# q and k turned into blocks of 32 adjacent values, with the order of time restored in products, masks and copies

## The chip, the cores and the metric

The kernel runs on one core of one Trainium2 chip. The core's engines run side by side, each with a queue of its own and tied to the others by semaphores: TensorE (PE, matrix products; its loads of the stationary operand are shown as PEld), VectorE (DVE), ScalarE (ACT), GpSimd (POOL), and SyncE (SP), which here only issues transfers. SBUF is the working memory of 128 partitions; PSUM holds TensorE's results. The metric is the device time of one execution in microseconds (us), lower is better. A profile is one execution recorded by the hardware profiler.

## The reference

Two blocks follow one another. The first is gated linear attention over 768 steps, for 4 sequences and 8 heads of 48 channels:

```python
for t in range(S):
    state = alpha[:, :, t, :, None] * state + np.einsum('bhd,bhe->bhde', k[:, :, t], v[:, :, t])
    y[:, :, t] = np.einsum('bhd,bhde->bhe', q[:, :, t], state)
```

The second takes y with the heads side by side, as x of 384 channels:

```python
proj = x @ w_in
val, gate = (proj[..., :D_inner], proj[..., D_inner:])
a = np.exp(A_log)[None, None, :]
h = np.zeros((B, D_inner), dtype=np.float32)
for t in range(S):
    h = a[0, 0] * h + val[:, t, :]
    ys[:, t, :] = h
silu = gate * (1.0 / (1.0 + np.exp(-gate)))
return (silu * ys @ w_out).astype(np.float32)
```

D_inner is 512. All inputs of the attention are fp32; the weights come as 64-bit floats and are converted on the chip.

## The kernel before

The 4 x 768 steps are cut into 12 groups of 256 steps (`GC`), numbered 0 to 11, three to a sequence. Everything is fp32. In SBUF, channels lie on partitions: heads 0 to 3 on partitions 0 to 47, heads 4 to 7 on 64 to 111, with 256 steps of each of the four heads of a half along the partition.

The recurrence becomes products. For a group, two scans on VectorE run over the gates alpha: P (line 635), the running product from the group's start, and V (line 654), from each step to the group's end, scaled by the reciprocal of the last P. The scaled queries Zq = q * P (`scaled_q`, line 610) and the scaled keys Zk = k * V (`scaled_k`, line 619) then go to TensorE:

- `scores` (line 797): for each head and each run of 64 steps (`L`), Zk is the stationary operand and Zq the moving one. In front of each 64 queries lie 48 columns of the identity, so one instruction of 112 columns gives the 64x64 scores and also turns k back to steps on partitions.
- `masks` (lines 807 to 817): the scores are multiplied by a triangular mask on VectorE or GpSimd into A, and the turned k is copied by ScalarE.
- `values` (line 831; for group 0 `first_values`, line 915): y from A and v. `carried` (line 844; group 0: line 923): y from the state before each run of 64 and Zq.
- `states` (line 863): the states' increments, summed by `add_up` on GpSimd (line 883) or `add_banks` on VectorE (line 891).
- `join` (lines 957 to 962; group 0: `first_join`): ScalarE copies y from PSUM; transfers issued by SyncE and GpSimd (line 960) bring each head to its place in xT, the input of the second block.
- `project` (line 981) multiplies xT with the weights, VectorE scans h from the result (`hh`, line 988), ScalarE makes the gate (line 999), VectorE or GpSimd multiplies both (line 1001). `output` (line 1015; for the last group line 1267) is the last product.

The inputs arrive with steps on partitions: partition c holds steps 8c to 8c+7 (`NJ` = 8 steps, 48 channels each, j counting the 8). Three ways turn them. Group 0's alpha and q have routines of their own on TensorE. Groups 0 to 2 of q and k, and alpha up to group 3, are turned by TensorE into PSUM and copied out by ScalarE (`turned` and `copy_turned`, lines 701 to 713). From group 3 for q and k, and group 4 for alpha, VectorE turns 32x32 blocks (`turn`, line 600): a block holds the 32 values of c for one j, and the result is written with 8 words between neighbours, so that the 256 steps lie in the order of time (8c + j).

The order of instructions on each engine is written out by hand in `fast`; every queue works in that order. `constants` fills, among others, the identity columns of the two Zq buffers (line 517) and the mask (line 524), both on GpSimd, and then issues the loads of group 0's v from GpSimd. For groups 0 and 2 `scaled_k` and `scaled_q` are called in halves (`c` = 0 and 1), each 512 values per partition; for all others whole, 1024 values. Weights are converted in between: by ScalarE (line 543), VectorE (lines 549 and 551) and GpSimd (line 556). Around this code stands a slower general version, taken only if the inputs are out of range; its instructions are not executed here.

Of the kernel before, what the change touches and what calls it, by code (L numbers as in the profile page):

```python
# [9 lines left out]
FP32 = mybir.dt.float32  # L10
# [3 lines left out]
AF = mybir.ActivationFunctionType  # L14
# [332 lines left out]
def fast(  # L347
# [39 lines left out]
    const = pool("const", 1)  # L387
    p1 = pool("p1", 1)
    p2 = pool("p2", 2)
# [4 lines left out]
    L = 64  # L394
    GP = GC + 1
    NJ = GC // 32
    ROW = NJ * D
    NQ = D + 16
    raws = {n: const.tile([C, 4 * ROW + 32], FP32, name=f"raw_{n}") for n in "aqk"}
# [83 lines left out]
    als = [const.tile([C, 4 * GP + 1], FP32, name=f"al{i}") for i in range(2)]  # L483
# [10 lines left out]
    def constants():  # L494
        make_identity(nc, ident)
        nc.vector.memset(wide_S[0], 0.0)
        for name in "aqk":
            for m in range(2):
                nc.vector.memset(steps_of(name, m)[:, 2 * ROW:], 1.0)
        for c in range(G):  # L500
            nc.vector.memset(wide[:, c].rearrange("p (h d) -> p h d", d=D)[:, 1::2, :], 0.0)
        for al in als:
            nc.vector.memset(al[:, ::GP], 0.0)
        nc.vector.memset(minus, -1.0)
        nc.vector.memset(one, 1.0)
        nc.vector.memset(lower, FLOOR)
        nc.vector.memset(lower[:, :, 0], FIRST_PRODUCT)
        nc.vector.memset(ends, 0.0)
        for t in wide_S[1:]:
            nc.vector.memset(t.rearrange("p (h d) -> p h d", d=D)[:, 1::2, :], 0.0)  # L510
        nc.scalar.activation(spare, minus, AF.Exp)
        for t in vs:
            nc.vector.memset(t[:, :, :, D:64], 0.0)
        for n, t in enumerate(Zqs):
            for i in range(2):
                rows = ds(64 * i, 64)
                nc.gpsimd.tensor_copy(out=t[rows, :, :, 0:D].rearrange("p u h d -> p (u h) d"),
                                      in_=ident[rows, None, ds(64 * i, D)].to_broadcast([64, 8 * G, D]))
            if n:
                nc.gpsimd.memset(tri, 1.0)  # L520
                nc.gpsimd.affine_select(out=tri, in_=tri, compare_op=ALU.is_ge, fill=0.0, base=0,
                                        channel_multiplier=-1, pattern=[[1, C]])
                for h in range(2):
                    nc.gpsimd.tensor_copy(out=mask[ds(L * h, L)], in_=tri[ds(L * h, L), ds(L * h, L)])
                load_v(0, nc.gpsimd)

    def bits_of(i):
# [65 lines left out]
    def by_place(t):  # L593
        return t[:, 0:4 * GP].rearrange("p (h t) -> p h t", h=4)

    def by_runs(t):
        return t.rearrange("p h (c j) -> p h c j", j=NJ)

    def turn(name, to):
        nc.vector.transpose(out=by_runs(to).rearrange("p h c j -> p h j c"),  # L600
                            in_=raws[name][:, 0:4 * ROW].rearrange("p (h j d) -> p h j d", h=4, d=D)
                            [:, :, :, 0:32])

    def plain(name):
        return p1.tile([C, 4, GC], FP32, tag=name, name=name)

    def scaled_q(m, t, P, c=None):
        u0, n = (0, 2 * G) if c is None else (2 * c, 2)
        at = ds(u0 * L, n * L)
        nc.vector.tensor_mul(Zqs[m % 2][:, ds(u0, n), :, D:].rearrange("p u h t -> p h u t"),  # L610
                             t[:, :, at].rearrange("p h (u t) -> p h u t", t=L),
                             P[:, :, 1:GP][:, :, at].rearrange("p h (u t) -> p h u t", t=L))

    def scaled_k(m, t, V, c=None):
        if not c:
            Zks[m] = p2.tile([C, G, 4, C], FP32, tag="Zk", name="Zk")
        c0, n = (0, G) if c is None else (c, 1)
        at = ds(c0 * C, n * C)
        nc.vector.tensor_mul(Zks[m][:, ds(c0, n)].rearrange("p c h t -> p h c t"),  # L619
                             t[:, :, at].rearrange("p h (c t) -> p h c t", t=C),  # L620
                             V[:, :, 1:GP][:, :, at].rearrange("p h (c t) -> p h c t", t=C))

    Zks = {}

# [85 lines left out]
    halves = [range(0, NJ // 2), range(NJ // 2, NJ)]  # L710

    def copy_turned(to, js, tp):
        nc.scalar.activation(by_runs(to)[:, :, :, js.start:js.stop], tp, AF.Copy)

    def first_alphas():
        raw, to = steps_of("a", 0), by_runs(by_place(als[0])[:, :, 1:GP])
# [66 lines left out]
    NS = S // L  # L783
    xTs, Ss, scs, sts, ys, partss = {}, {}, {}, {}, {}, {}

    def scores(m, cs=range(G)):
        Zk, Zq = Zks[m], Zqs[m % 2]
        for c in cs:
            scs.setdefault(m, []).append(bank_pair(None if c else "s"))
            if not c or not m:  # L790
                sts.setdefault(m, []).extend(scs[m][c])
            for p in range(4):
                for h in range(2):
                    u = 2 * c + h
                    for i in range(2):
                        rows = ds(64 * i, D)
                        nc.tensor.matmul(scs[m][c][i][ds(L * h, L), ds(p * (L + D), L + D)],  # L797
                                         Zk[rows, c, p, ds(h * L, L)], Zq[rows, u, p],
                                         start=True, stop=True, skip_group_check=True)

    def masks(m, cs=range(G)):
# [33 lines left out]
    def carried(m, us):  # L835
        for u in us:
            j = (m % NG) * 2 * G + u - 1
            if j < 0:
                continue
            for e in range(2):  # L840
                for s in range(2):
                    for i in range(2):
                        p, rows = 2 * e + (s ^ i), ds(64 * i, D)
                        nc.tensor.matmul(ys[m][i][ds(64 * s, 64), e, ds(u * L, L)], Ss[j][rows, p, :],  # L844
                                         Zqs[m % 2][rows, u, p, D:], start=False, stop=True,
                                         skip_group_check=True)

    def states(m):
# [69 lines left out]
    def first_carried(us):  # L918
        for u in us:
            for pair in zip(spread(0), spread(1)):  # L920
                for i, (p, at, to, e) in enumerate(pair):
                    rows = ds(64 * i, D)
                    nc.tensor.matmul(ys[0][i][to, e, ds(u * L, L)], wide_S[u - 1][rows, ds(at, L)],
                                     Zqs[0][rows, u, p, D:], start=False, stop=True, skip_group_check=True)

    def first_states(st):
        to = [t.rearrange("p (h d) -> p h d", d=D)[:, ::2, :] for t in wide_S]
# [3 lines left out]
        for u in range(1, 4):  # L931
            nc.vector.tensor_add(to[u], st[u % 2][u // 2], to[u - 1])

    def first_join():
        y = ys.pop(0)
        xT = xTs[0] = p2.tile([C, NK, GC], FP32, tag="xT", name="xT")
        nc.scalar.activation(xT[:, 0], y[0][:, 0], AF.Copy)
        nc.scalar.activation(xT[0:64, 1], y[0][0:64, 1], AF.Copy)
        nc.scalar.activation(xT[64:128, 1], y[1][64:128, 0], AF.Copy)
        nc.scalar.activation(xT[:, 2], y[1][:, 1], AF.Copy)  # L940

    moves = []
    for h in range(H):
        i, e, s = h // 4, h % 4 // 2, h % 2 ^ h // 4
        at = D * h
# [7 lines left out]
    def join(m, engines):  # L953
        y = ys.pop(m)
        st = p1.tile([C, 2, 2, GC], FP32, tag="yst", name="yst")
        xT = xTs[m] = p2.tile([C, NK, GC], FP32, tag="xT", name="xT")
        nc.scalar.activation(st[:, 0], y[0], AF.Copy)  # L957
# [89 lines left out]
    P = scan_P(0)  # L1047
# [3 lines left out]
    V = scan_V(0, P, False)  # L1051
# [17 lines left out]
    st = states(0)  # L1069
# [10 lines left out]
    P = scan_P(1)  # L1080
# [33 lines left out]
    for n in range(N):  # L1114
        m = n + 1
        if n == 0:
# [12 lines left out]
            P = scan_P(2)  # L1129
# [176 lines left out]
```

## Time and profile before

| | |
|---|---|
| time, median of 3 runs | 275.85 us (275.72 to 275.88) |
| profiled execution, span from first to last instruction | 274.0 us; the runs' median is 1.85 above it |
| PE busy | 269.2 us (98%), 4060 matrix products |
| DVE busy | 217.9 us (80%), 271 instructions |
| ACT busy | 109.5 us (40%) |
| POOL busy | 123.7 us (45%) |
| the chain that ended last | PE 91%, DVE 5%, ACT 1%, POOL 1%, issue 1% |

The profile gives no time of its own for the execution beside the span. A row of the groups reads: line, engine, operation, output<-inputs, shape, count | busy us in all, mean ns of one | us that the engine was idle just before them, and what ended it. A row of a timeline reads: start us, duration us, engine, line, operation, output<-inputs, count, and in brackets the idle time before it with what ended it. "PE busy" counts modelled ends of pipelined matrix products: products of one run overlap, so what a run costs is read from the start of one to the start of the next.

### The profile page before, as it was taken

The numbers are of one execution on the slowest core, as the hardware profiler recorded it, in microseconds if no ns is written. First come the engines' busy times: TensorE is split into PE (matmuls) and PEld (weight loads), VectorE is DVE, ScalarE is ACT, GpSimd is POOL, SyncE is SP. The second block draws the span as 40 slices with busy tenths as digits, with TensorE's granted clock in tenths as the row PEclk, the third lists the DMA queues.
The fourth block names the chain that finished last, engine by engine and source line by source line (L and its number), as shares of the span: only waits on it lengthen the run. The fifth ranks groups of instructions, "written<-read, shape, count | busy, mean of one in ns | idle before, by whom it ended". The sixth has DMA issues, their size and how long they took to land.

```text
span 274.0 us, 9640 instructions
## 1 busy us (share of the span) xinstructions
PE 269.2 (98%) x4060; PEld 216.8 (79%) x4060; DVE 217.9 (80%) x271; ACT 109.5 (40%) x252; POOL 123.7 (45%) x144
## 2 busy tenths in 40 slices
PE   8999999999999999999999999999999999999995
PEld 6988888876788687788688688688688787787884
DVE  7979998996798999694995995996995995873240
ACT  3668766451344333524424424425425415213111
POOL 8122223260237485385384485376376476334000
PEclk9999999999999999999999999999999999999999
DMA  6948975989639686684585595585596501201201
GB/s 173 319 141 263 265 169 160 260 174 226 167 97 229 162 192 147 178 190 119 151 204 135 150 208 137 143 208 138 137 214 144 138 0 31 73 1 38 70 2 60
DMA packets 52303, 41.18 MB, mean 150 GB/s; under 512 B 27392, under 2 KB 50944, under 8 KB 52256
## 3 DMA queue, kind: packets, MB, share of 16 engines
q1 hardware_dynamic: 49328, 37.34, 53.9%
q0 software_dynamic: 1536, 2.20, 3.0%
q10 hardware_dynamic: 1392, 0.99, 1.2%
q8 instruction: 33, 0.54, 0.9%
q14 instruction: 14, 0.11, 0.1%
HBM read 32.54 MB, written 4.72 MB: 136 GB/s over the span
## 4 chain that ended last, share of the span: by engine, by line
PE 91%; DVE 5%; issue 1%; ACT 1%; POOL 1%; DVEq 0%; POOLq 0%; ACTq 0%
PE mm L981 46%; PE mm L1015 21%; PE y L831 4%; PE y L844 4%; PE mm L797 3%; PE s L797 3%; PE s L863 3%; PE mm L1267 2%; DVE P L635 2%; PE mm L706 1%; PE y L778 1%; DVE V L654 1%; POOL w_in L556 1%; PE s L722 1%; DVE Zk L619 0%
## 5 line engine op out<-in xcount | busy, mean ns | idle before, releaser
L981 PE MATMUL mm<-xT,w_in 128*128 128x256 f32 x576 | 129.5, 382 | 0.1
L981 PEld LDWEIGHTS mm<-xT,w_in 128*128 128x128 f32 x576 | 107.9, 190 | 16.2 <-POOL w_in L556 0.4
L1015 PE MATMUL mm<-w_out,f_last 128*128 128x384 f32 x160 | 54.2, 492 | 0.0
L999 ACT ACTIVATE sg<-mm 128x256 f32<-128x256 f32 x48 | 18.4, 383 | 86.7 <-PE mm L981 86.6
L1001 POOL TENSOR_TENSOR f_last<-sg,hh 128x256 f32<-128x256 f32 x36 | 32.9, 917 | 33.4 <-ACT sg L999 19.9
L1015 PEld LDWEIGHTS mm<-w_out,f_last 128*128 128x128 f32 x160 | 29.7, 190 | 19.7
L883 POOL TENSOR_TENSOR sum<-sum,dS 128x192 f32<-128x192 f32 x30 | 30.3, 1010 | 21.4 <-ACT dS L871 11.9
L988 DVE TENSOR_TENSOR_SCAN hh<-a_dec,hh,mm 128x256 f32<-128x256 f32 x32 | 23.4, 731 | 14.5 <-PE mm L981 14.2
L635 DVE TENSOR_TENSOR_SCAN P<-al,lower 128x1028 f32<-128x1028 f32 x12 | 31.4, 2617 | 0.5
L654 DVE TENSOR_TENSOR_SCAN V<-al,ends 128x1028 f32<-128x1028 f32 x12 | 28.3, 2360 | 0.4
L960 POOL DMA_DIRECT2D xT<-yst x44 | 22.5, 517 | 12.6 <-ACT yst L957 11.3
L1009 ACT ACTIVATE o_sb<-mm 128x384 f32<-128x384 f32 x22 | 10.8, 490 | 37.4 <-PE mm L1015 37.4
L815 POOL TENSOR_TENSOR AK<-AK,mask 128x512 f32<-128x512 f32 x9 | 15.2, 1683 | 18.7 <-ACT AK L813 18.7
L812 DVE TENSOR_TENSOR A<-s,mask 128x256 f32<-128x256 f32 x9 | 3.8, 424 | 19.5 <-PE s L797 19.5
L556 POOL TENSOR_TENSOR w_in<-w_in,wr 128x768 int32<-128x768 int32 x4 | 7.3, 1825 | 25.6 <-DVE wr L551 16.1
L600 DVE STREAM_TRANSPOSE k<-raw_k 128x1024 f32<-128x1024 f32 x9 | 18.3, 2034 | 0.0
L600 DVE STREAM_TRANSPOSE q<-raw_q 128x1024 f32<-128x1024 f32 x9 | 18.2, 2019 | 0.0
L600 DVE STREAM_TRANSPOSE al<-raw_a 128x1024 f32<-128x1024 f32 x8 | 16.3, 2042 | 0.0
L619 DVE TENSOR_TENSOR Zk<-k,V 128x1024 f32<-128x1024 f32 (+1 forms) x14 | 16.1, 1150 | 0.1
L831 PEld LDWEIGHTS y<-AK,v 64*64 64x64 f32 x352 | 12.1, 134 | 5.1 <-issue 5.1
L610 DVE TENSOR_TENSOR Zq<-q,P 128x1024 f32<-128x1024 f32 (+1 forms) x14 | 14.8, 1056 | 0.1
L831 PE MATMUL y<-AK,v 64*64 64x64 f32 x352 | 14.5, 221 | 0.0
(163 smaller groups left out, 389.2 us busy)
## 6 DMA issues: line engine op xcount, KB each, us to landing
v<-in_v_dram SPq DMA_DIRECT2D x22, 192.0 KB, 3.4
out_dram<-o_sb SPq DMA_DIRECT2D x22, 192.0 KB, 2.5
raw_k<-in_k_dram SPq DMA_DIRECT2D x18, 184.0 KB, 3.4
raw_q<-in_q_dram SPq DMA_DIRECT2D x18, 184.0 KB, 3.8
raw_k<-in_k_dram SPq DMA_DIRECT2D x18, 176.0 KB, 3.7
raw_q<-in_q_dram SPq DMA_DIRECT2D x18, 176.0 KB, 4.0
wbits<-in_moe_w_in_dram SPq DMA_DIRECT2D x8, 384.0 KB, 5.7
raw_a<-in_alpha_dram SPq DMA_DIRECT2D x16, 184.0 KB, 5.0
```

The lines of the kernel that those rows point to most:

```text
L600: nc.vector.transpose(out=by_runs(to).rearrange("p h c j -> p h j c"), in_=raws[name][:, 0:4 * ROW].rearrange("p (h j d) -> p h j d", h=4, ...
L635: nc.vector.tensor_tensor_scan(out=P, data0=al[:, 0:4 * GP], data1=lower.rearrange("p h t -> p (h t)"), initial=0.0, op0=ALU.mult, op1=ALU ...
L654: nc.vector.tensor_tensor_scan(out=V[:, ::-1], data0=al[:, 1:4 * GP + 1][:, ::-1], data1=ends.rearrange("p h t -> p (h t)")[:, ::-1], init ...
L797: nc.tensor.matmul(scs[m][c][i][ds(L * h, L), ds(p * (L + D), L + D)], Zk[rows, c, p, ds(h * L, L)], Zq[rows, u, p], start=True, stop=True ...
L831: nc.tensor.matmul(ys[m][i][ds(64 * s, 64), e, ds(c * C + h * L, L)], v_sb[rows, c, 4 * i + p, :], As[i][rows, c, p, :], start=across and ...
L883: nc.gpsimd.tensor_add(Ss[j][:, :, 0:D], Ss[j - 1][:, :, 0:D], part)
L960: engines[n % len(engines)].dma_start(out=xT[to, a], in_=st[rows, i, e])
L981: nc.tensor.matmul((pv, pg)[vg], w_ins[cc][:, kk, vg, :], xT[:, kk, :], start=(kk == 0), stop=(kk == NK - 1))
L988: nc.vector.tensor_tensor_scan(out=hh, data0=a_dec[:, cc:cc + 1].to_broadcast([C, GC]), data1=pv, initial=prev_h[cc][:, GC - 1:GC] if n % ...
L999: nc.scalar.activation(sg, pg, AF.Silu)
L1001: f = lambda: engine.tensor_mul(fs[n][cc], sg, hh)
L1015: nc.tensor.matmul(os[c], fs[n][cc][:, ds(c * C, C)], w_outs[cc // 2][:, cc % 2, :], start=(cc == 0), stop=(cc == NI - 1))
```

## The change

q and k are no longer put in the order of time when they are turned. A turned tensor (`plain`) has the shape (head, j, c): for each of the 8 j the 32 values of c lie side by side, as the turn makes them. Alpha keeps the order of time, and so do P and V.

- `turn` writes its result as it comes for q and k; for alpha the caller passes the old pattern, steps of 8 words.
- `copy_turned` (ScalarE, out of PSUM) writes q and k in runs of 32 and reads PSUM in the other order.
- `scaled_k` multiplies the turned k, read across (one value, then the one 32 words on), with V in the order of time; Zk is in the order of time.
- `scaled_q` multiplies the turned q, read in runs, with P read 8 words apart. Zq keeps the order (j, c): 14 rows of 32 words for each head, 6 of identity columns and 8 of queries.
- A run of 64 steps is 8 neighbouring c for all 8 j, so `queries` gives TensorE 8 (or, with the identity, 14) runs of 8 words, 32 words apart. Within each 64 steps, the columns of the scores and of y are in the order (j, c).
- The mask gets its columns in that order. ScalarE's copies of y (`first_join`, `join`) read PSUM at steps of 8 words and write the order of time.
- The identity columns are written by 16 GpSimd copies of 192 values per partition instead of 4 of 768.

Number and order of the other instructions are as before on every engine. The diff, cut to its core:

```diff
-    Zqs = [const.tile([C, 2 * G, 4, L + D], FP32, name=f"Zq{i}") for i in range(2)]
+    Zqs = [const.tile([C, 4, NR + NJ, 32], FP32, name=f"Zq{i}") for i in range(2)]
...
-                nc.gpsimd.tensor_copy(out=t[rows, :, :, 0:D].rearrange("p u h d -> p (u h) d"),
-                                      in_=ident[rows, None, ds(64 * i, D)].to_broadcast([64, 8 * G, D]))
+                for u in range(2 * G):
+                    nc.gpsimd.tensor_copy(
+                        out=t[rows, :, 0:NR, ds(NJ * u, NJ)],
+                        in_=ident[rows, None, ds(64 * i, D)].to_broadcast([64, 4, D])
+                        .rearrange("p h (a c) -> p h a c", c=NJ))
...
-                    nc.gpsimd.tensor_copy(out=mask[ds(L * h, L)], in_=tri[ds(L * h, L), ds(L * h, L)])
+                    nc.gpsimd.tensor_copy(out=mask[ds(L * h, L)].rearrange("p (j c) -> p j c", j=NJ),
+                                          in_=tri[ds(L * h, L), ds(L * h, L)].rearrange("p (c j) -> p j c", j=NJ))
...
+    def of_runs(t):
+        return t.rearrange("p h (c j) -> p h j c", j=NJ)
+
     def turn(name, to):
-        nc.vector.transpose(out=by_runs(to).rearrange("p h c j -> p h j c"),
+        nc.vector.transpose(out=to,
...
-        return p1.tile([C, 4, GC], FP32, tag=name, name=name)
+        return p1.tile([C, 4, NJ, 32], FP32, tag=name, name=name)
...
-        nc.vector.tensor_mul(Zqs[m % 2][:, ds(u0, n), :, D:].rearrange("p u h t -> p h u t"),
-                             t[:, :, at].rearrange("p h (u t) -> p h u t", t=L),
-                             P[:, :, 1:GP][:, :, at].rearrange("p h (u t) -> p h u t", t=L))
+        at = ds(0, 32) if c is None else ds(16 * c, 16)
+        nc.vector.tensor_mul(Zqs[m % 2][:, :, NR:, at], t[:, :, :, at], of_runs(P[:, :, 1:GP])[:, :, :, at])
...
-            Zks[m] = p2.tile([C, G, 4, C], FP32, tag="Zk", name="Zk")
...
+            Zks[m] = p2.tile([C, 4, GC], FP32, tag="Zk", name="Zk")
+        at = ds(0, 32) if c is None else ds(16 * c, 16)
+        nc.vector.tensor_mul(by_runs(Zks[m])[:, :, at], t.rearrange("p h j c -> p h c j")[:, :, at],
+                             by_runs(V[:, :, 1:GP])[:, :, at])
...
-        turn("a", by_place(als[m % 2])[:, :, 1:GP])
+        turn("a", of_runs(by_place(als[m % 2])[:, :, 1:GP]))
...
-        nc.scalar.activation(by_runs(to)[:, :, :, js.start:js.stop], tp, AF.Copy)
+        if len(to.shape) == 3:
+            nc.scalar.activation(by_runs(to)[:, :, :, js.start:js.stop], tp, AF.Copy)
+        else:
+            nc.scalar.activation(to[:, :, js.start:js.stop], tp.rearrange("p h c j -> p h j c"), AF.Copy)
...
+    def queries(m, u, p, i, first=NR):
+        return Zqs[m % 2][ds(64 * i, D), p, first:, ds(NJ * u, NJ)]
...
-                                         Zk[rows, c, p, ds(h * L, L)], Zq[rows, u, p],
+                                         Zk[ds(64 * i, D), p, ds(u * L, L)], queries(m, u, p, i, 0),
...
-                                         Zqs[m % 2][rows, u, p, D:], start=False, stop=True,
+                                         queries(m, u, p, i), start=False, stop=True,
...
+    def steps_of_y(t):
+        return t.rearrange("p (u j c) -> p u c j", j=NJ, c=NJ)
+
+    def to_steps(t):
+        return t.rearrange("p (u c j) -> p u c j", j=NJ, c=NJ)
...
-        nc.scalar.activation(st[:, 0], y[0], AF.Copy)
-        nc.scalar.activation(st[:, 1], y[1], AF.Copy)
+        for i in range(2):
+            nc.scalar.activation(to_steps(st[:, i].rearrange("p e t -> p (e t)")),
+                                 steps_of_y(y[i].rearrange("p e t -> p (e t)")), AF.Copy)
...
-            nc.scalar.activation(xT[to, a], y[i][rows, e], AF.Copy)
+            nc.scalar.activation(to_steps(xT[to, a]), steps_of_y(y[i][rows, e]), AF.Copy)
```

More of the change, by code (lines that the diff above doesn't have):

```diff
@@ L396, in fast @@
     NJ = GC // 32
+    NR = D // NJ
     ROW = NJ * D
@@ L784, in fast @@
     xTs, Ss, scs, sts, ys, partss = {}, {}, {}, {}, {}, {}
+    def queries(m, u, p, i, first=NR):
+        return Zqs[m % 2][ds(64 * i, D), p, first:, ds(NJ * u, NJ)]
     def scores(m, cs=range(G)):
-        Zk, Zq = Zks[m], Zqs[m % 2]
+        Zk = Zks[m]
         for c in cs:
@@ L795, in scores @@
                     for i in range(2):
-                        rows = ds(64 * i, D)
                         nc.tensor.matmul(scs[m][c][i][ds(L * h, L), ds(p * (L + D), L + D)],
-                                         Zk[rows, c, p, ds(h * L, L)], Zq[rows, u, p],
+                                         Zk[ds(64 * i, D), p, ds(u * L, L)], queries(m, u, p, i, 0),
                                          start=True, stop=True, skip_group_check=True)
@@ L923, in first_carried @@
                     nc.tensor.matmul(ys[0][i][to, e, ds(u * L, L)], wide_S[u - 1][rows, ds(at, L)],
-                                     Zqs[0][rows, u, p, D:], start=False, stop=True, skip_group_check=True)
+                                     queries(0, u, p, i), start=False, stop=True, skip_group_check=True)
     def first_states(st):
@@ L936, in first_join @@
         xT = xTs[0] = p2.tile([C, NK, GC], FP32, tag="xT", name="xT")
[L937 to L940, printed above, removed]
+        for to, of in ((xT[:, 0], y[0][:, 0]), (xT[0:64, 1], y[0][0:64, 1]),
+                       (xT[64:128, 1], y[1][64:128, 0]), (xT[:, 2], y[1][:, 1])):
+            nc.scalar.activation(to_steps(to), steps_of_y(of), AF.Copy)
     moves = []
```

7 lines of the change are left out of this document (removed).

## The prediction

> **What bounds the kernel now.** I read the page's busy line and its chain of waits, then busy time by stage, then the engines' timelines at the places where TensorE stands.
>
> ```profile
> span 274.0 us, 9640 instructions
> PE 91%; DVE 5%; issue 1%; ACT 1%; POOL 1%; DVEq 0%; POOLq 0%; ACTq 0%
> ```
>
> ```profile
> 27.40:45.00 17.60, 17.59 (x425) 15.65 (x426) 16.59 (x27) 11.84 (x24) 4.48 (x4) 1.00 0.79 214
> 45.00:72.00 27.00, 27.00 (x291) 20.25 (x293) 23.41 (x33) 10.64 (x24) 7.42 (x9) 1.00 0.86 205
> 72.00:255.00 183.00, 182.92 (x2775) 145.28 (x2768) 149.34 (x156) 67.12 (x160) 101.36 (x114) 1.00 0.56 136
> ```
>
> In these rows the first number after the stretch is its length and the second TensorE's busy time. From 27.4 to 255 us TensorE is idle 0.09 us in all: there, a faster VectorE can give back at most that. Only the first 27.4 us are a chain through VectorE, ScalarE and GpSimd; whatever is added there moves everything behind it. The clock is 1.00 throughout. The span is 274.0 us, the median of the runs 275.85, so 1.85 us lie around the span, and I add my sum to both.
>
> **The change, part by part.**
>
> *The turns.* 18 VectorE transposes (groups 3 to 11, q and k) now write 32 adjacent values instead of values 8 words apart; the eight turns of alpha stay as they are.
>
> ```profile
> L600 DVE STREAM_TRANSPOSE k<-raw_k 128x1024 f32<-128x1024 f32 x9 | 18.3, 2034 | 0.0
> L600 DVE STREAM_TRANSPOSE q<-raw_q 128x1024 f32<-128x1024 f32 x9 | 18.2, 2019 | 0.0
> L549 DVE TENSOR_SCALAR w_in<-wbits 128x768 uint32<-128x768 uint32 x4 | 2.2, 542 | 0.0
> ```
>
> ```profile
> 81.09 1.22 DVE L619 TENSOR_TENSOR Zk<-k,V 128x1024 f32<-128x1024 f32 x1
> 82.23 0.74 DVE L988 TENSOR_TENSOR_SCAN hh<-a_dec,hh,mm 128x256 f32<-128x256 f32 x1
> 82.89 2.02 DVE L600 STREAM_TRANSPOSE q<-raw_q 128x1024 f32<-128x1024 f32 x1
> 84.76 0.67 DVE L988 TENSOR_TENSOR_SCAN hh<-a_dec,hh,mm 128x256 f32<-128x256 f32 x1
> 85.36 1.21 DVE L610 TENSOR_TENSOR Zq<-q,P 128x1024 f32<-128x1024 f32 x1
> ```
>
> From start to next start the turn of 1024 values takes 84.76-82.89 = 1.87 us and the packed product 82.23-81.09 = 1.14. If the scattered write is the reason for the difference, a turn saves 0.73; if it is something in the turn itself, nothing. I take 0.73: 18 x 0.73 = 13.1 us of VectorE, none of it on TensorE's path, by the stage rows above.
>
> *The products with the gates.* Their data is now read against its order: Zq's product reads P 8 words apart (32 bytes), Zk's reads the turned k 32 words apart, one value at a time; the other operand and the output keep runs. There are 14 of each (ten full, four halves). No row of before shows such a read. Lower end: no price; the L549 row reads every second word and takes 542 ns for 768, 0.7 ns per value against the packed product's 1.1, so a small step is free. Upper end: a GpSimd product of two inputs, 1.83 us for 768 (row at 25.52 below), 2.4 ns per value, so 2.4x1024 less 1.14 = +1.3 us per full product and +0.6 per half. I take the row with the like step on the same engine, the turn's write: +0.73 per full product and +0.37 per half. So the cost moves: per group two turns give 1.46 back and two products take 1.46. Groups 0 to 2 are turned by TensorE and only pay.
>
> [...]
>
> *Where it lies on the path: group 0.*
>
> ```profile
> 6.66 2.30 DVE L635 TENSOR_TENSOR_SCAN P<-al,lower 128x1028 f32<-128x1028 f32 x1
> 9.21 2.30 DVE L654 TENSOR_TENSOR_SCAN V<-al,ends 128x1028 f32<-128x1028 f32 x1
> 11.61 0.69 DVE L619 TENSOR_TENSOR Zk<-k,V 128x512 f32<-128x512 f32 x1
> 12.22 0.68 DVE L610 TENSOR_TENSOR Zq<-q,P 128x512 f32<-128x512 f32 x1
> 13.43 0.68 DVE L610 TENSOR_TENSOR Zq<-q,P 128x512 f32<-128x512 f32 x1
> 14.16 0.42 DVE L807 TENSOR_TENSOR A<-s,mask 128x256 f32<-128x256 f32 x1
> ```
>
> ```profile
> 14.26 1.00 PE L797 MATMUL mm<-Zq,Zk 48*64 48x112 f32 x32 [0.20 <-ACT k L713]
> ```
>
> Four halves in a row, 0.61 apart; the last ends at 14.11 and the second scores start 0.15 later. The copy that the profile names there ends at 14.20, so it covers nothing worth counting once the products are late. 4 x 0.37 = +1.5 us.
>
> *Groups 1 and 2.*
>
> ```profile
> 25.86 2.58 DVE L619 TENSOR_TENSOR Zk<-k,V 128x1024 f32<-128x1024 f32 x1
> 28.36 1.21 DVE L610 TENSOR_TENSOR Zq<-q,P 128x1024 f32<-128x1024 f32 x1
> 29.49 0.67 DVE L988 TENSOR_TENSOR_SCAN hh<-a_dec,mm 128x256 f32<-128x256 f32 x1
> 42.79 0.68 DVE L610 TENSOR_TENSOR Zq<-q,P 128x512 f32<-128x512 f32 x1
> ```
>
> ```profile
> 25.52 1.83 POOL L556 TENSOR_TENSOR w_in<-w_in,wr 128x768 int32<-128x768 int32 x1 [6.15 <-DVE wr L551]
> ```
>
> ```profile
> 30.19 0.78 PEld L797 LDWEIGHTS s<-Zq,Zk 48*64 48x64 f32 x32 [0.33 <-DVE hh L988]
> ```
>
> ```profile
> 43.83 0.95 PE L797 MATMUL mm<-Zq,Zk 48*64 48x112 f32 x32
> ```
>
> Group 1's Zk is 2.58 long because it stands until GpSimd's instruction ends at 27.35, then runs 1.09: the two engines exclude each other. Its pair of products gets 2 x 0.73 = 1.5 longer. Zq then ends at 31.0 instead of 29.57; TensorE had 0.5 us to spare (30.19 less 29.57 and about 0.1), so it loses 1.0. VectorE itself is 1.5 late and is busy without a gap to the next products, so group 2's four halves start 1.5 late and take 1.5 longer: its last Zq ends at 43.47+3.0 and its scores start 0.15 behind, at 46.6 instead of 43.83, +2.8 (this holds group 1's 1.0). Behind them the masks, sums and h scans queue, equally late.
>
> *GpSimd's constants.* Four copies of 768 values become sixteen of 192 (same bytes), ahead of the mask and the loads of v in its queue.
>
> ```profile
> 1.52 3.44 POOL L517 COPY Zq<-ident 64x768 f32<-64x768 f32 x4
> 5.66 0.50 POOL L524 COPY mask<-tri 64x64 f32<-64x64 f32 x2
> 6.11 1.94 POOL L441 DMA_DIRECT2D wide<-in_v_dram  x2
> 83.79 0.34 POOL L881 COPY sum<-dS 128x192 f32<-128x192 f32 x1
> 136.81 2.35 POOL L881 COPY sum<-dS 128x192 f32<-128x192 f32 x1 [4.49 <-ACT dS L871]
> ```
>
> ```profile
> 136.72 2.30 DVE L654 TENSOR_TENSOR_SCAN V<-al,ends 128x1028 f32<-128x1028 f32 x1
> ```
>
> A copy of 192 takes 0.34, with gaps some 0.375: 16 x 0.375 = 6.0, so they end at 7.5 instead of 4.96, and the P scan starts at 6.66 between them. A copy under a scan waits for its end (the 2.35 row: 136.81 to the V scan's end at 139.02, and 0.14 more), and Zk's row showed the reverse. Taking turns, about two copies (0.34 each, less the slack before V), the select for the mask and its two copies fall between P, V and the products: about +1.2 us on the path, since the first mask product needs the mask. Ends: nothing if the copies finish before 6.66; 2.5 if each costs 0.45 and five stand over. The loads of v would be issued near 16 us instead of 6.11, when few other loads run; I take nothing for them, and 1.5 us at the upper end.
>
> *From group 3 on* turn and product cancel. The tightest place is group 4, whose Zq ends at 86.57, 0.15 before TensorE needs it:
>
> ```profile
> 86.72 1.00 PE s L797 x32
> ```
>
> Two turns and two products lie ahead of it, 2 x (0.73-0.73) = 0.
>
> *At nothing:* ScalarE's copies now read PSUM against its order.
>
> ```profile
> L713 ACT ACTIVATE k<-mm 128x512 f32<-128x512 f32 x6 | 3.6, 598 | 1.3 <-PE mm L702 0.6 <-DVE Zk L619 0.5 <-PE mm L706 0.3
> L957 ACT ACTIVATE yst<-y 128x512 f32<-128x512 f32 x11 | 6.6, 597 | 10.9 <-PE y L844 7.3 <-DMA raw_q<-in_q_dram 3.1 <-ACT sg L999 0.6
> ```
>
> The k copy reads PSUM 128 words apart today and takes 598 for 512; the packed copy of y 597. The masks only hold other values; instruction counts on TensorE, the order on all queues and all DMAs stay. TensorE now streams q in runs of 8 words, 32 apart: no row shows it. Lower end nothing; upper end the turn's ratio 1.87/1.14 on 24 batches of scores of 0.95 (row at 43.83), +15. I take nothing.
>
> Sum: 1.5 + 1.2 + 2.8 = 5.5; span 279.5, time **281.4 us**.
>
> **The rivals.**
>
> A, not slower: reads at a step are free on VectorE and the copies end before the scan. For it: the L549 row, and that only a write at a step is shown slow. Then nothing on the path gets longer and the turns are off it: 275.85 less at most 0.09 = 275.8. It decides if a half product stays near 0.68. With free reads but the constants in the way: 277.0.
>
> B: reads are dearer than the turn's write, 2.4 ns per value. Start 2.4+1.2, groups 1 and 2 2x1.3+4x0.6-0.2 = 4.8, and group 4's Zq late by 2x(1.3-0.73) = 1.1: +9.5, 285.4; with dear copies and late v up to 287.5.
>
> C: the turns get no faster (the change doesn't do what it says): groups 0 to 2 as forecast, and group 4 loses 2 x 0.73 more: 282.8. Against: packed VectorE rows run at 1.14.
>
> D: TensorE slows on runs of 8 words. A tenth on 24 x 0.95 us is +2.3, with the carried products, which read the same runs, about +3: 284.4; the full upper end 296. [...]
>
> **How the numbers follow.** The forecast has 0.62, A 0.12 (0.03 faster, 0.05 no change, 0.04 slower through the constants), B 0.13, C 0.08, D 0.05. Faster or slower starts at 0.2%, 0.55 us, about what this measurement can tell. The likeliest case's own range is 279.5 to 283.5 (constants 0 to 2.5, prices a tenth either way). The range leaves out A below and the ends of B and D above: 278.0 to 287.0.
>
> **What would show it.** Right: turns of q and k near 1.2 us, alpha's still 2.04; full products near 2.0, halves near 1.05; the second scores of group 0 near 17.0; stands before group 1's and 2's scores; TensorE's L797 group still 256 ns; GpSimd's small copies 0.34, the last ones held by the scans. Wrong: halves at 0.68 (A), products above 2.4 (B), turns at 2.0 (C), scores' matmuls longer (D).

## The result and the profile after

The changed kernel takes 283.97 us (median of 4 runs, 282.77 to 285.13), the kernel before 275.79 (275.39 to 275.88): a ratio of 1.029, 95% interval 1.025 to 1.033. The profiled execution took 282.77, with a span of 281.0 against 274.0, so 7.0 us are to be explained; the other three took 283.3, 284.6 and 285.1.

The groups of instructions of the changed kernel (columns as before):

```profile
L608 DVE STREAM_TRANSPOSE q<-raw_q 128x1024 f32<-128x1024 f32 x9 | 11.0, 1226 | 0.0
L608 DVE STREAM_TRANSPOSE al<-raw_a 128x1024 f32<-128x1024 f32 x8 | 16.3, 2042 | 0.0
L623 DVE TENSOR_TENSOR Zk<-k,V 128x1024 f32<-128x1024 f32 x10 | 20.8, 2075 | 0.0
L617 DVE TENSOR_TENSOR Zq<-q,P 128x1024 f32<-128x1024 f32 x10 | 20.2, 2020 | 0.1
L623 DVE TENSOR_TENSOR Zk<-k,V 128x512 f32<-128x512 f32 x4 | 4.4, 1090 | 0.1
L805 PE MATMUL mm<-Zq,Zk 48*64 48x112 f32 x384 | 11.6, 257 | 1.9 <-DVE Zq L617 1.9
L719 ACT ACTIVATE k<-mm 128x512 f32<-128x512 f32 x6 | 3.6, 598 | 2.2 <-DVE Zk L623 1.6 <-PE mm L705 0.6
```

The turns of q and k went from 2.02 to 1.23 us, those of alpha stayed at 2.04. The full products went from 1.21 (row at 85.36 of before) to 2.02, the halves from 0.68 to 1.09. TensorE's products are as long as they were (257 ns against 256), and so are ScalarE's copies (598). What is new is in TensorE's idle column: 1.9 us before the scores, ended by Zq.

The chain of work that ended last, after (start us, duration us, what):

```profile
15.60 1.17 PE mm L805 x32
...
30.52 2.01 DVE Zq L617
...
32.57 1.00 PE s L805 x32
...
47.02 1.00 DVE Zq L617
48.07 1.00 PE mm L805 x32
49.07 4.46 PE mm L995 x12
53.53 0.62 PE y L839 x32
...
77.89 0.93 PE s L805 x32
...
91.20 2.29 POOL sum L891
...
93.54 0.46 PE y L852 x16
...
95.54 5.36 PE mm L1029 x16
```

and the same view of the kernel before, at places that the prediction doesn't show:

```profile
44.77 2.79 PE mm L981 x12
47.56 0.62 PE y L831 x32
...
71.52 0.93 PE s L797 x32
...
88.48 5.36 PE mm L1015 x16
```

Set side by side, the lateness of the changed kernel grows like this:

| place | before | after | late by | of that new |
|---|---|---|---|---|
| group 0, second scores | 14.26 | 15.60 | 1.34 | 1.34: four half products, 1.59 longer in all, begun 0.24 earlier (11.37) |
| group 1, first scores | 30.20 | 32.57 | 2.37 | 1.03: two full products |
| group 2, second scores | 43.83 | 48.07 | 4.24 | 1.87: VectorE's lateness and four halves |
| end of the 12 projection products behind them | 47.56 | 53.53 | 5.97 | 1.73: half clock (the 12 take 4.46 instead of 2.79) |
| group 3, first scores | 71.52 | 77.89 | 6.37 | 0.40: one stop of TensorE, without a known cause |
| group 4, output products behind the scores | 88.48 | 95.54 | 7.06 | 0.69: GpSimd's sum |
| end of the span | 274.0 | 281.0 | 7.0 | -0.06 |

The 0.24 of the first row is scatter of the start: VectorE's first scan of P begins at 6.66 in the kernel before, at 6.85 in the experiment pause and at 7.17 in pause_half, which have the same code up to there. In the changed kernel it begins at 6.34 and the second scores start at 15.60; in the experiment warm, again the same code up to there, they start at 16.30. Behind group 4 nothing is added in 185 us.

Three of these rows are not in the prediction. The first is the clock. Busy time by stage, after (length; busy share and count of PE, PEld, DVE, ACT, POOL; granted TensorE clock; DMA share; GB/s):

```profile
45.00:46.00 1.00, 0.61 (x44) 0.47 (x34) 1.00 (x3) 0.34 (x1) 0.00 (x0) 1.00 1.02 406
46.00:47.00 1.00, 0.83 (x32) 0.81 (x32) 1.00 (x3) 1.00 (x3) 0.45 (x1) 1.00 0.55 213
47.00:48.00 1.00, 0.17 (x8) 0.00 (x0) 1.00 (x3) 0.38 (x2) 1.00 (x3) 1.00 0.30 78
48.00:49.00 1.00, 0.93 (x33) 0.79 (x33) 0.68 (x3) 0.62 (x2) 0.62 (x2) 1.00 0.37 98
49.00:50.00 1.00, 1.00 (x6) 0.83 (x3) 0.88 (x3) 0.47 (x3) 0.00 (x0) 0.51 0.30 74
50.00:51.00 1.00, 1.00 (x4) 0.81 (x3) 0.89 (x3) 0.24 (x1) 0.00 (x0) 0.50 0.75 107
51.00:52.00 1.00, 1.00 (x4) 0.82 (x3) 1.00 (x1) 0.00 (x0) 0.00 (x0) 0.50 0.60 200
52.00:53.00 1.00, 1.00 (x5) 0.83 (x5) 1.00 (x2) 0.00 (x0) 0.00 (x0) 0.79 1.04 424
```

TensorE stood for 0.39 + 0.17 + 0.83 + 0.07 = 1.46 us between 45 and 49; then it was granted half its clock for 0.98 + 1 + 1 + 0.42 = 3.4 us, and gave up half of that, 1.7. The mean clock of the four runs is 0.994, 0.994, 0.987 and 0.987: one such stretch of 3.4 us in 281 gives 0.994, two give 0.988. That fits the difference between the runs at 283 and those at 285; only one of the four was profiled, so the second stretch is inferred.

The second is small. The 48 carried products of y in the second half of group 2 take 0.40 longer. TensorE's timeline, before and after:

```profile
54.94 0.88 PE L844 MATMUL y<-Zq,sum 48*64 48x64 f32 x48
...
60.91 1.28 PE L852 MATMUL y<-Zq,sum 48*64 48x64 f32 x48
```

The profile names nothing that TensorE waited for there. Of the experiments below, g2 and warm have a stop of TensorE at the same place (0.06 us between 61 and 62 and 0.41 between 63 and 64), while in the chains of h012, g0 and g1 these products take 0.70, as in that of before (1.10 in that of after). The cause stays open.

The third is at group 4. The timelines of GpSimd and VectorE there, after,

```profile
90.54 2.95 POOL L891 TENSOR_TENSOR sum<-sum,dS 128x192 f32<-128x192 f32 x2
90.97 2.06 DVE L617 TENSOR_TENSOR Zq<-q,P 128x1024 f32<-128x1024 f32 x1
```

and before:

```profile
84.21 1.28 POOL L883 TENSOR_TENSOR sum<-sum,dS 128x192 f32<-128x192 f32 x2
```

Before, both sums of GpSimd were all but done (85.49) when VectorE's Zq product began (85.36). In the changed kernel the shorter turn lets Zq begin 0.43 us after the sums instead of 1.15; Zq takes 2.06, to 93.03; the second sum, 2.29 long where the first takes 0.59, ends at 93.49. TensorE's carried products (L852) wait 0.76 us for the sum.

### The profile page after: what moved, and what is told of

The parts are those of the page before. It is cut to its first block, busy times and chain, and to the rows that moved or that the text cites. A ratio compares the mean times of both kernels' runs of the same rounds, so it can differ in the third digit from the quotient of the medians.

```text
span 281.0 us, 9653 instructions
## 1 busy us (share of the span) xinstructions
PE 271.4 (97%) x4060; PEld 217.8 (78%) x4060; DVE 222.5 (79%) x271; ACT 109.8 (39%) x252; POOL 134.0 (48%) x156
## 4 chain that ended last, share of the span: by engine, by line
PE 80%; DVE 14%; issue 3%; POOL 1%; ACT 1%; DVEq 0%; POOLq 0%
PE mm L995 40%; PE mm L1029 21%; PE y L839 4%; PE y L852 4%; PE mm L805 4%; PE s L805 3%; DVE Zk L623 3%; PE s L871 3%; DVE Zq L617 2%; DVE P L638 2%; PE mm L1281 2%; DVE V L657 2%; PE mm L709 1%; POOL sum L891 1%; DVE hh L1002 1%
## 5 line engine op out<-in xcount | busy, mean ns | idle before, releaser
L995 PE MATMUL mm<-xT,w_in 128*128 128x256 f32 x576 | 131.1, 386 | 0.1
L995 PEld LDWEIGHTS mm<-xT,w_in 128*128 128x128 f32 x576 | 109.2, 192 | 16.6 <-POOL w_in L561 0.4
L891 POOL TENSOR_TENSOR sum<-sum,dS 128x192 f32<-128x192 f32 x30 | 37.9, 1263 | 21.7 <-ACT dS L879 12.1
L1015 POOL TENSOR_TENSOR f_last<-sg,hh 128x256 f32<-128x256 f32 x36 | 32.2, 900 | 28.7 <-ACT sg L1013 20.3
L657 DVE TENSOR_TENSOR_SCAN V<-al,ends 128x1028 f32<-128x1028 f32 x12 | 27.6, 2304 | 0.4
L623 DVE TENSOR_TENSOR Zk<-k,V 128x1024 f32<-128x1024 f32 (+1 forms) x14 | 25.1, 1794 | 0.1
L617 DVE TENSOR_TENSOR Zq<-q,P 128x1024 f32<-128x1024 f32 (+1 forms) x14 | 24.6, 1754 | 0.1
L971 ACT ACTIVATE yst<-y 128x512 f32<-128x512 f32 x22 | 11.9, 595 | 12.3 <-PE y L852 7.1
L852 PEld LDWEIGHTS y<-Zq,sum 48*64 48x64 f32 x656 | 11.8, 134 | 4.7 <-issue 2.8
L852 PE MATMUL y<-Zq,sum 48*64 48x64 f32 x656 | 14.5, 222 | 0.9 <-POOL sum L891 0.8
```

Source lines behind the costliest of these rows:

```text
L617: nc.vector.tensor_mul(Zqs[m % 2][:, :, NR:, at], t[:, :, :, at], of_runs(P[:, :, 1:GP])[:, :, :, at])
L623: nc.vector.tensor_mul(by_runs(Zks[m])[:, :, at], t.rearrange("p h j c -> p h c j")[:, :, at], by_runs(V[:, :, 1:GP])[:, :, at])
L657: nc.vector.tensor_tensor_scan(out=V[:, ::-1], data0=al[:, 1:4 * GP + 1][:, ::-1], data1=ends.rearrange("p h t -> p (h t)")[:, ::-1], init ...
L891: nc.gpsimd.tensor_add(Ss[j][:, :, 0:D], Ss[j - 1][:, :, 0:D], part)
L995: nc.tensor.matmul((pv, pg)[vg], w_ins[cc][:, kk, vg, :], xT[:, kk, :], start=(kk == 0), stop=(kk == NK - 1))
L1015: f = lambda: engine.tensor_mul(fs[n][cc], sg, hh)
```

## The experiments

**The price of an access at a step, by itself (reads).** The kernel before, with products and turns of 1024 values behind its last work; its time says nothing.

```diff
+        nc.vector.tensor_mul(z, x, y)
+        for s in (2, 4, 8, 16, 32):
+            nc.vector.tensor_mul(packed(z, s), by(x, s), packed(y, s))
+        for s in (8, 32):
+            nc.vector.tensor_mul(packed(z, s), packed(x, s), by(y, s))
...
+        for s in (8, 32):
+            nc.vector.tensor_mul(by(z, s), packed(x, s), packed(y, s))
+        nc.vector.tensor_mul(packed(z, 8), by(x, 8), by(y, 8))
+        nc.vector.transpose(out=z, in_=x)
...
+        nc.vector.transpose(out=by(z, 8), in_=packed(x, 8))
```

> The kernel before with products and turns of 1024 values per partition added on VectorE behind everything else: packed; one input read at steps of 2, 4, 8, 16 and 32 words (first input), of 8 and 32 (second input); both inputs in runs of 2 words, 16 apart; output at steps of 8 and 32; both inputs at steps of 8; a packed turn, a turn of 32 blocks, a turn written at steps of 8. Theory, the price belongs to a read or write that takes one word and hops: packed 1.19 us, step 2 free, steps of 8 and 32 about 2.0 whichever input, runs of two words free, output at step 8 about 2.0, both inputs no dearer than one. Rival, the price comes from the number of dimensions: runs of two words cost as much as single words. The time of this kernel says nothing (about 30 us of added work).

The instructions of that part by line (count: shortest/median/longest ns, first and last start). L1254 is the first line of the diff, all packed; L1256 has the first input at a step of 2, 4, 8, 16 and 32 words, L1258 the second at 8 and 32, L1259 both in runs of two words (left out of the diff), L1263 the output at 8 and 32, L1264 both inputs at 8; L1265 and L1267 are the two turns shown:

```profile
L1256 DVE TENSOR_TENSOR raw_a<-raw_q,raw_k x10: 1224/1902/2016, 268.6 to 302.1; 128x1024 f32<-128x1024 f32 x10
L1258 DVE TENSOR_TENSOR raw_a<-raw_q,raw_k x4: 1919/1959/2004, 277.8 to 306.1; 128x1024 f32<-128x1024 f32 x4
L1263 DVE TENSOR_TENSOR raw_a<-raw_q,raw_k x4: 1889/1951/2000, 283.0 to 311.3; 128x1024 f32<-128x1024 f32 x4
L1254 DVE TENSOR_TENSOR raw_a<-raw_q,raw_k x2: 1224/1224/1225, 267.3 to 293.6; 128x1024 f32<-128x1024 f32 x2
L1259 DVE TENSOR_TENSOR raw_a<-raw_q,raw_k x2: 1226/1226/1226, 281.8 to 308.0; 128x1024 f32<-128x1024 f32 x2
L1264 DVE TENSOR_TENSOR raw_a<-raw_q,raw_k x2: 1995/1997/1999, 287.0 to 313.3; 128x1024 f32<-128x1024 f32 x2
L1265 DVE STREAM_TRANSPOSE raw_a<-raw_q x2: 1245/1246/1247, 289.0 to 315.3; 128x1024 f32<-128x1024 f32 x2
L1267 DVE STREAM_TRANSPOSE raw_a<-raw_q x2: 2015/2015/2015, 291.6 to 317.8; 128x1024 f32<-128x1024 f32 x2
```

A product is 1.22 us packed, with one input at every second word, or with both inputs in runs of two words. It is 1.89 to 2.02 as soon as single words lie 4 or more apart, on either input (L1256 from a step of 4 on, L1258), on the output (L1263) or on both inputs at once (L1264). A turn is 1.25 packed and 2.02 with a scattered output. So the price belongs to the access, not to reading or writing, and not to the turn; the turn's write was the right row to take, as far as these steps of 4 to 32 words go. Per value the scattered products take 1.85 to 1.97 ns, the packed one 1.20.

**The first three groups left in the order of time (h012).** Groups 0 to 2 of q and k as before, 3 to 11 as changed; the tiles of Zq are seen in both layouts, and the second mask and the new identity columns are written between groups 1 and 4.

```diff
+    IN_TIME = (0, 1, 2)
...
     def scaled_q(m, t, P, c=None):
+        if m in IN_TIME:
...
+            return
         at = ds(0, 32) if c is None else ds(16 * c, 16)
```

> Groups 0 to 2 of q and k stay in the order of time (packed products, as in the kernel before); groups 3 to 11 are as changed, and GpSimd writes the blocks' identity columns and mask later, between groups. My theory: all of the loss but about 0.9 us comes from the products of groups 0 to 2 and from the clock that falls behind their pauses; group 4 keeps its wait for GpSimd's sums. 276.7 us, clock 1.00. Rival, the loss is spread over all groups (TensorE on runs of 8 words, or turn and product not cancelling): 278 to 281. Rival, the wait at group 4 is a result of the later start: 275.8.

276.53 us (276.11 to 277.02, 10 runs) beside 276.09 of the kernel before on the same chip: ratio 1.0018 [1.0004, 1.0033], clock 0.999 to 1.00. The changed kernel took 8.2 us more than the kernel before measured beside it, this one 0.4 more: all but 0.4 comes with groups 0 to 2, and nine groups of cheaper turns and dearer products cost no more than that. What is left of the loss shows in its chain at group 4, the same sum of GpSimd:

```profile
85.10 2.28 POOL sum L924
...
87.42 0.46 PE y L885 x16
```

**One of the three groups at a time (g0, g1, g2, g12).** The same kernel, with a shorter list: (1, 2) in g0, whose diff is shown, (0, 2) in g1, (0, 1) in g2 and (0,) in g12; and the identity columns and masks written where the first group of each layout needs them.

```diff
-    IN_TIME = (0, 1, 2)
+    IN_TIME = (1, 2)
```

> Groups 3 to 11 and, of the first three, group 0 alone are in the new layout. Theory (each pause costs its own length, and the half clock needs pauses that lie close together): group 0's second scores 1.34 us late as in the changed kernel, no stretch of half clock, 276.5 + 1.3 = 277.8 us. Rival (TensorE's clock falls after any pause of about a microsecond): one stretch of half clock, worth 1.7 us more, 279.5.

280.0 us (278.78 to 282.02, 4 runs), ratio 1.0174 [1.0121, 1.0227]. Two runs kept the clock at 1.00 and took 278.8 and 278.9; the others had 0.993 and 0.988 and took 281.1 and 282.0. The second scores start at 15.58, as in the changed kernel. The missing 1.1 us up to 278.9 are my kernel's own: GpSimd rewrites identity columns beside group 2's products, and two of these take 1.27 and 1.31 instead of 0.68. Neither expectation held in all runs. The long pauses of this kernel are those of group 0 (0.59 and 1.00 us, 13.0 to 15.58), and half clock came in two executions and stayed away in two; the profiled one has 1.00 throughout, so the place is inferred.

> Groups 3 to 11 and group 1 alone. Theory: one pause of 0.9 us before group 1's scores, no half clock, 276.5 + 1.0 = 277.5 us; group 2's products start 1.5 us later than in the kernel with groups 0 to 2 in order of time, which may add up to 0.5. Rival: half clock after this pause, 279.2.

278.2 us (277.99 to 278.35), ratio 1.0085 [1.0068, 1.0102], clock 0.998 to 1.00. That is 2.3 over the kernel before on its chip, 1.8 more than h012 lost, where 1.0 to 1.5 was expected. Group 1's scores are 0.83 later than in h012, group 2's 1.12. There was no half clock, but TensorE stood only 0.26 us ahead of group 1's scores instead of the 0.9 expected, so this run doesn't test what such a pause does to the clock.

> Groups 3 to 11 and group 2 alone. Theory: four half products of 0.40 us more each, less what the products had to spare, 276.5 + 1.6 = 278.1 us at most, no half clock. Rival: half clock after this pause, 279.8.

> Groups 3 to 11 and groups 1 and 2. Theory (the pauses of groups 1 and 2, 0.86, 0.56 and 0.90 us within 16 us, are what brings the clock down): 276.5 + 2.9 of pauses + 1.7 of half clock = 281.1 us. Rival (group 0's pause takes part in it, or the clock does not depend on how near the pauses are): 279.4.

283.25 us (283.06 to 283.36; 1.0269 [1.0252, 1.0286]) and 283.96 us (283.02 to 284.57; 1.0286 [1.0258, 1.0315]), clocks 0.986 to 0.994. These two don't measure group 2's products: they need new identity columns in a tile that group 0 has just used, and the scores wait for those copies. TensorE's timeline in g2:

```profile
44.01 0.40 PE L838 MATMUL s<-Zq,Zk 48*64 48x112 f32 x2 [1.09 <-POOL Zq L542]
46.15 1.86 PE L838 MATMUL s<-Zq,Zk 48*64 48x112 f32 x29 [1.73 <-POOL Zq L542]
```

They tell of the clock alone: with pauses like these, longer than those of the changed kernel, it was 0.994 or less in all eight runs. The question they were made for, whether the pauses of groups 1 and 2 by themselves bring the clock down, stays open.

**A pause and nothing else (pause, pause_half).** The kernel before, with idle writes of 256 zeros on VectorE ahead of group 2's products: twelve in pause, whose diff is shown, five in pause_half.

```diff
             load_v(3, nc.sync)
+            for n_pad in range(12):
+                nc.vector.memset(pad, 0.0)
             for c in range(G):
                 scaled_k(2, tk, V, c)
```

> The kernel before with 12 memsets of 256 values (0.27 us each, 3.3 us) on VectorE ahead of group 2's products, nothing else changed. Theory, a pause costs twice, by itself and by the clock: 3.1 us for the later scores plus 1.7 for one stretch of half clock, 280.6 us, clock 0.994. Rival, the clock falls only through what the changed kernel does on TensorE: 278.9 us, clock 1.00.

> The kernel before with 5 memsets of 256 values (0.27 us each, 1.4 us) on VectorE ahead of group 2's products. Theory, TensorE's pause there is about 1 us, like those of the changed kernel; +1.2 us for the later scores, and in some executions 1.7 more for half clock: 277.3 to 279. Rival, a pause of 1 us never costs clock: 277.3, clock 1.00 in all.

pause: 282.63 us (281.63 to 283.26), ratio 1.0226 [1.0193, 1.0259], clock 0.994 in one run and 0.988 in three. Its busy time by stage:

```profile
46.00:47.00 1.00, 0.00 (x0) 0.00 (x0) 1.00 (x3) 0.00 (x0) 0.41 (x1) 0.72 0.37 95
47.00:48.00 1.00, 0.90 (x20) 0.93 (x24) 1.00 (x2) 0.00 (x0) 0.00 (x0) 0.50 0.40 99
...
53.00:54.00 1.00, 1.00 (x5) 0.89 (x4) 1.00 (x2) 0.00 (x0) 0.00 (x0) 0.86 1.11 240
```

Half clock from 46.4 to 53.3, two stretches of 3.4 us where I had expected one. With q and k in their old layout, a pause alone brought the clock down to 0.50. This pause was longer than those of the changed kernel: TensorE stood 3.0 us before the clock fell. pause_half: 277.72 us (277.07 to 278.32), ratio 1.0058 [1.0034, 1.0082], clock 0.998 to 1.00. TensorE stood 0.27 + 0.69 + 0.11 = 1.07 us there:

```profile
43.00:44.00 1.00, 0.73 (x52) 0.59 (x41) 0.88 (x4) 0.22 (x1) 0.00 (x0) 1.00 0.95 381
44.00:45.00 1.00, 0.31 (x13) 0.34 (x17) 1.00 (x2) 1.00 (x3) 0.33 (x1) 1.00 0.73 284
45.00:46.00 1.00, 0.89 (x39) 0.67 (x32) 1.00 (x3) 0.49 (x2) 1.00 (x3) 1.00 0.24 64
```

**Work to fill the pauses (warm, warm2).** The changed kernel, with TensorE products whose results are overwritten ahead of the scores: zeros in groups 1 and 2, then (the diff shown) the identity matrix in all five pauses.

```diff
+            for _ in range({(0, 0): 6, (0, 1): 8, (1, 0): 5, (2, 0): 4, (2, 1): 7}.get((m, c), 0)):
+                nc.tensor.matmul(scs[m][c][0][:, 0:C], ident, ident, start=True, stop=True,
+                                 skip_group_check=True)
```

> The changed kernel with dummy matmuls of zeros in TensorE's pauses ahead of the scores of groups 1 and 2 (3, 2 and 4 of 256 columns); the real scores overwrite what they leave. My theory: the granted clock falls to half for about 3.4 us because TensorE stood still there; with the dummies it stays 1.00 and the pauses themselves remain: 281.7 us, and the runs agree within 0.5 us. Rival, the clock falls for another reason (load, chance): still 284 with a clock of 0.987 to 0.994.

> The changed kernel with dummy matmuls (identity by identity, 128 columns: 6, 8, 5, 4 and 7 of them, 0.11 us each) in TensorE's pauses ahead of the scores of groups 0, 1 and 2; the real scores overwrite what they leave. Theory, the clock falls when TensorE stands still for much of some stretch, and which of the pauses does it is chance: with all five pauses filled it stays 1.00, the pauses remain, 281 to 282 us, and the runs agree within 1 us. Rival, the clock falls for another reason: a clock of 0.987 to 0.994 and 284 us or more.

warm: 285.73 us (285.18 to 287.39), clock 0.988 to 0.994. In the profiled execution the clock stayed at 1.00 at group 2 and fell at group 0, where no work was added; and six pieces of added work ahead of group 1's scores cost 1.47 us. warm2: 285.19 us; four of six runs at clock 1.00 took 284.9 to 285.3, two at 0.994 took 287.5 and 287.7. Both missed on time: the added work starts too late to be hidden. One row of TensorE's timeline in warm2 shows it, ahead of scores that then start at 17.83 instead of 15.60:

```profile
15.85 2.05 PE L802 MATMUL mm<-ident 128*128 128x128 f32 x16
```

The changed kernel kept its clock in none of four runs, warm2 in four of six. What follows is only that with this work in the pauses the clock was kept more often, and that the work cost more than the 1.7 us it saved.

**The constants alone (small).** The kernel before, with its four identity copies on GpSimd cut into sixteen; columns and mask stay in the order of time.

```diff
-                nc.gpsimd.tensor_copy(out=t[rows, :, :, 0:D].rearrange("p u h d -> p (u h) d"),
-                                      in_=ident[rows, None, ds(64 * i, D)].to_broadcast([64, 8 * G, D]))
+                for u in range(2 * G):
+                    nc.gpsimd.tensor_copy(out=t[rows, u, :, 0:D],
+                                          in_=ident[rows, None, ds(64 * i, D)].to_broadcast([64, 4, D]))
```

> The kernel before with only GpSimd's identity columns written by 16 copies of 192 values instead of 4 of 768, everything else as before. The prediction's price: +1.2 us (277.2). What the profile of the changed kernel suggests: the scans get in first and GpSimd waits, +0.1 to 0.2 us (276.1).

276.18 us beside 276.02, ratio 1.0003 [0.9991, 1.0016]: no price that can be measured. GpSimd's timeline in the changed kernel shows why:

```profile
1.52 5.00 POOL L519 COPY Zq<-ident 64x192 f32<-64x192 f32 x16
...
6.86 1.91 POOL L525 TENSOR_SCALAR_AFFINE_SELECT tri<-tri 128x128 f32<-128x128 f32 x1
8.82 2.54 POOL L528 COPY mask<-tri 64x64 f32<-64x64 f32 x2
```

The copies follow each other at 0.31 us instead of 0.375 and end at 6.52. What then meets VectorE's scans waits for them: the select takes 1.91 where the one at 1.17, of the same shape, takes 0.29, and ends at 8.77, 0.10 behind the scan of P; and the masks are there at 11.36, while the first mask product needs them only behind the half products, at 15.4.

**Group 4's product cut in two (h012_split4).** The kernel h012, so that GpSimd's sum can come between the halves of Zq.

```diff
-        scaled_q(m, tq, P)
+        if m in (4,):
+            for c in range(G):
+                scaled_q(m, tq, P, c)
+        else:
+            scaled_q(m, tq, P)
```

> As the kernel with groups 0 to 2 in the order of time, and group 4's product of q made in two halves, so that GpSimd's sum can run between them. Theory, TensorE's wait of 0.8 to 1.0 us at group 4 is GpSimd's second sum standing behind the product of 2 us: with halves it waits at most 1.1 us, and 0.5 to 0.9 us come back: 275.6 to 276.0, level with the kernel before. Rival, the wait is for something else: 276.5 as without the split.

277.0 us (275.56 to 277.66, 11 runs; a twelfth, with a clock of 0.992, took 280.7), ratio 1.0023 [0.9999, 1.0046]: not better. GpSimd's timeline:

```profile
84.33 2.03 POOL L928 TENSOR_TENSOR sum<-sum,dS 128x192 f32<-128x192 f32 x2
...
90.98 2.57 POOL L928 TENSOR_TENSOR sum<-sum,dS 128x192 f32<-128x192 f32 x1
93.52 1.25 POOL L860 TENSOR_TENSOR AK<-AK,mask 128x512 f32<-128x512 f32 x1
```

The two sums at group 4 now take 2.03 instead of 2.9, and their wait is gone from the chain; some 7 us later a sum that takes 0.59 elsewhere takes 2.57, beside one VectorE instruction that fills the time from 91 to 93 without a gap (by the order of the code the scan of P), and holds up a mask and, behind it, TensorE until 94.83. That the wait at group 4 was for the sum is shown by this; the collision moved on. No version faster than the kernel before was found.

## Why the prediction was right, and where it was off

It said slower, 281.4 us in a range of 278.0 to 287.0; the median is 283.97, the profiled execution 282.77. The way and the path were right: the dearer products of groups 0 to 2 make TensorE stand. The likeliest case had a range of its own, 279.5 to 283.5; the median lies above that, in the room that was left for rivals B and D, which did not come. By its steps:

- *Turns* (0.73 less each): right in sign and nearly in size, 0.79 to 0.82; the write was the cause, as the row by itself shows (1.25 against 2.02).
- *Products* (0.73 more, 0.37 for a half): 0.8 and 0.40. The choice of the turn's write as the nearest row was the step that carried the forecast. No row then showed that a read costs the same as a write; the experiment on access showed it afterwards. Neither bound came, free reads or 2.4 ns.
- *Group 0's half products* (+1.5): 1.59 longer; with a start 0.24 earlier, +1.34 in all.
- *GpSimd's constants* (+1.2): wrong, nothing measurable. The second scores of group 0, expected near 17.0 with this term, started at 15.60. The working let a copy under a scan cost the path; the trace shows GpSimd waiting, the scans 2.33 and 2.35 long instead of 2.30, and slack of about 4 us before the masks are needed. The gap between small copies was taken too long as well.
- *Groups 1 and 2* (+2.8): +2.9. What group 1's scores lose, put at 1.0, was 1.03.
- *Group 4* (turn and product cancel, nothing): the cancelling held for Zq, but the path there was not Zq's. A VectorE product of 2.06 us instead of 1.21, begun 0.4 us into GpSimd's sums, kept the second sum waiting: +0.7. The prediction named only Zq's own slack at this place and not the engine beside it, although it had read that very exclusion off group 1's Zk.
- *The clock*: the prediction's sum has no term for it. The prediction read "the clock is 1.00 throughout" off the kernel before and put pauses at their own length. A stretch of half clock (3.4 us at 0.50) cost 1.7 us; there is one in the profiled execution and, by the mean clock, two in others.
- *ScalarE's copies and TensorE's runs of 8 words* at nothing: right, 598 and 257 ns.

The forecast's 5.5 us stands against 5.3 without the clock, but partly by luck: 1.2 too many at the constants cancel 0.7 too few at group 4 and the 0.40 of the stop behind group 2, which has no explanation here. With the clock's 1.7 it is the 7.0 of the profiled execution, and a second stretch would make up the slower runs.

Of the rivals, free reads (A) and reads at 2.4 ns (B) fell with the rows of the experiment on access; turns that get no faster (C) and a slower TensorE stream (D) fell with the groups after, D also because nothing is added behind group 4. By the time alone they could not have been told apart: D stood at 284.4.

## What to carry to other kernels

Here a rearrangement was moved from one instruction to the next, and its price moved with it: a VectorE instruction of 1024 values paid 0.65 to 0.8 ns per value once (1.89 to 2.02 us against 1.22 packed), whichever of its operands hopped by 4 to 32 words, and so the question was only which of the two instructions lay on the path in the stages where VectorE set the pace. A forecast that adds pauses to the busiest engine should add what they do to its clock: here one or two times 1.7 us on 5.3. And an instruction that gets longer on VectorE should be looked at together with what GpSimd does at that moment, since it may be GpSimd's result that TensorE waits for (0.76 us here, at group 4).

## What the runs showed of the hardware beyond the prediction

The granted clock. It fell to 0.50 for 3.4 us or twice that, after TensorE had stood, in the few microseconds before, for 1.46 us (changed kernel, group 2), 1.68 (g2), 1.76 (g12), 1.79 (warm2, in group 0's carried products, where the profile names nothing that TensorE waited for), 1.97 (warm, group 0) or 3.0 (pause). It did not fall after 1.07 (pause_half, mean clock 0.998 to 1.00 in all five runs), nor in the profiled execution after 0.86 (changed kernel, group 1) or 1.70 (the same, group 0); g0, with group 0's pauses, lost it in two runs of four. So the time that TensorE stood does not by itself tell whether the clock falls: group 0's 1.70 lies within 2.7 us and kept the clock, group 2's 1.46 lies within 2.5 and lost it. A second stretch of 3.4 us came, in the profiled executions, where TensorE went on standing after the fall (pause 0.67 us, g12 0.84, g2 1.15), and none came where it did not (changed kernel, warm, warm2). How long TensorE has to stand before the clock falls, and why executions of one kernel differ, no run here shows.

The second hopping operand cost nothing: 1.997 us with both inputs at a step of 8 words against 2.00 with one. And where GpSimd was seen waiting for VectorE, its instruction came second and ended shortly behind VectorE's: a select took 1.91 us instead of 0.29 under a scan and ended 0.10 behind it, the scan taking 2.33 instead of 2.30; group 4's second sum took 2.29 instead of 0.59 and ended 0.46 behind Zq's product. The other way round, in the changed kernel group 1's Zk took 3.27 us where group 4's took 1.96, beside a GpSimd product that began 0.34 ahead of it and ended at 28.80.
